# Column-group matmuls for the first MLP layer and the query projection of a decode block

## The chip, the cores and the metric

The kernel runs on one core of a Trainium2 chip. The metric is the device time of one execution in microseconds (us), the median of several executions. The span that a profile covers is about 1.8 us shorter than the time (133.4 against 135.22 us for the profiled run of the kernel before), because the time also includes a start and an end.

The words used below: PE is the matrix engine, DVE the vector engine, ACT the scalar engine, POOL a further engine that hardly works here; SP issues the large loads. HBM is the large memory that the DMA engines read from, SBUF the memory on the core that they write to, PSUM the memory that receives the results of matmuls. A matmul has a stationary operand, which is loaded into PE first (a weight load), and a moving operand, whose columns are then streamed through. The granted clock is the share of its full clock that PE was given, as the profile records it.

## The reference

One token (a row of 576 numbers) goes through two branches, and a gate mixes them:

```python
q = x @ wq                               # [576] x [576, 4096], 32 heads of 128
k, v = k_cache[:, :, -4096:], v_cache[:, :, -4096:]   # 16 heads x 4096 x 128, bf16
p = softmax(q k^T / sqrt(128))           # two query heads share one k/v head
a = (p v) @ wo                           # [4096] x [4096, 576]
h = gelu(x @ w1 + b1)                    # [576] x [576, 4608]
b = h @ w2 + b2                          # [4608] x [4608, 576]
g = sigmoid(sum(x * gate_w))
out = g * a + (1 - g) * b
```

Each weight is used once and each cache entry for two query heads at once, so no load can be saved by reuse. The windows of K and V are 2 x 16 x 4096 x 128 x 2 bytes = 33.6 MB, the four weight matrices 20.1 MB. The profile shows 53.62 MB read from HBM.

## The kernel before

All large loads are issued in order from one engine (SP) into a few large buffers, which are tagged A to D and used again:

```python
w1_t = big.tile([P, NI, FH], ..., tag="B")      # 3 DMAs, 5.3 MB
wq_t = big.tile([P, NI, QH], ..., tag="A")      # 3 DMAs, 4.7 MB
# ...
for g in range(NG):
    k_t = big.tile([P, 2, SL, Dh], ..., tag="CDBA"[g])   # K group 2 needs w1's buffer, group 3 wq's
    # ... per half group: DVE transposes 128x2048 twice into kt (2 buffers), PE 16 score matmuls
# ...
w2_t = big.tile([P, NF, D], ..., tag="B")       # first half of w2: needs K group 2 transposed
# v_t tags "CDAC"[g], wo_t tag "D", second half of w2 into w2_t
```

In MLP layer 1 the weight is the stationary operand and x the moving one. The 576 rows of w1 are cut into two halves of 2304 columns, which gives 1152 half rows, 9 (NI) on each partition. Column t of `x2[:, i, :]` holds x on those partitions whose half row i belongs to half t, and zeros elsewhere. The result lands on the partitions directly:

```python
h_ps = ps_m.tile([P, NF], FP32, name="h_ps", tag="m")
for j in range(NJ):                       # 18 bias matmuls
    nc.tensor.matmul(h_ps[:, j:NF:NJ], lhsT=b1_t[:, j:FH:NJ], rhs=ident[0:2, 0:2], ...)
for i in range(NI):
    for j in range(NJ):                   # 9 x 18 = 162 weight loads, 2 moving columns each
        nc.tensor.matmul(h_ps[:, j:NF:NJ], lhsT=w1_t[:, i, j:FH:NJ], rhs=x2[:, i, :], ...)
# ... gelu on h_ps
for i in range(NI):
    for j in range(Hq // 2):              # 9 x 16 = 144 for q, the same way
        nc.tensor.matmul(q_ps[:, j : Hq : Hq // 2], lhsT=wq_t[:, i, j * Dh : (j + 1) * Dh], rhs=x2[:, i, :], ...)
nc.vector.tensor_copy(out=q_b[:], in_=q_ps[:])
# ... 4 matmuls and 4 copies scatter q_b into the block-diagonal qz_flat, then the K stage starts
```

## Time and profile before

| | before |
|---|---|
| time, median of 3 | 135.37 us (135.1 to 135.47) |
| HBM read | 53.62 MB |
| DMA share of the chain that ended last | 71% |
| PE busy | 81.0 us, 61% of the span |
| MLP layer 1 on PE | 10.4 to 21.8 us |
| first K transpose on DVE | 30.70 us |

The first view is the profile page of the kernel before: the span in 40 slices of 3.3 us (busy tenths of PE, the granted PE clock in tenths, busy tenths of the 16 DMA engines, GB/s moved), then the chain of work that ended last, by engine and by line.

```profile
PE   0239999260957778768789185008923955296771
...
PEclk9999999999999999999999968655555555555798
DMA  4999999999999999999999999999998999999970
GB/s 137 416 437 419 422 452 400 415 418 442 432 413 437 417 435 418 432 427 405 435 444 474 442 393 418 472 432 393 432 467 373 403 408 441 407 420 422 408 266 0
...
DMA 71%; DVE 10%; ACT 7%; PE 6%; issue 2%; SPq 1%; DVEq 0%
DMA k_t<-in_A_k_cache_dram 25%; DMA w_t<-in_B_w_dram 18%; DMA wq_t<-in_A_wq_dram 15%; DMA v_t<-in_A_v_cache_dram 13%; ACT p_t L356 7%; DVE kt L305 5%; PE o_ps L400 3%; DVE pt L364 2%; DVE m L326 2%; PE s_ps L314 1%; SPq L281 1%; PE q_ps L242 1%; PE t_ps L382 0%; PE mb_ps L343 0%; DVE out_row L435 0%
```

The chain is mostly the DMA of K, w1 and w2 (both printed as w_t), wq and V; PE has 6% of it. GB/s stays between about 370 and 475 whether PE is busy or not. The clock row needs care: the first record of the granted clock in this trace is at 36.6 us, and slices before it are printed as full. The distance of the score matmuls' starts says otherwise: 427 ns before that record and 217 ns after it. So the scores from 33.1 us up to that record ran at the half clock; what the clock was before them, this trace does not show.

The second view is the busy time by stage, kernel before: start and end of the stage in us, its length, then busy time of PE, PE weight loads, DVE, ACT and POOL, each with its number of instructions, then granted clock, DMA share and GB/s.

```profile
core 0: us, PE busy (x) PEld busy (x) DVE busy (x) ACT busy (x) POOL busy (x), PEclk, DMA share, GB/s
...
4.00:16.00 12.00, 7.98 (x105) 6.83 (x106) 4.91 (x36) 0.17 (x1) 0.00 (x0) 1.00 1.01 427
16.00:32.00 16.00, 10.19 (x241) 9.96 (x241) 3.83 (x12) 0.75 (x3) 0.00 (x0) 1.00 1.01 423
32.00:76.00 44.00, 31.90 (x128) 12.59 (x127) 37.16 (x18) 0.00 (x0) 0.00 (x0) 1.00 1.01 430
...
92.00:112.00 20.00, 12.72 (x449) 12.27 (x447) 0.00 (x0) 0.00 (x0) 0.00 (x0) 0.50 0.99 418
112.00:128.00 16.00, 10.01 (x117) 5.90 (x118) 0.48 (x2) 0.00 (x0) 0.00 (x0) 0.58 1.01 419
```

In none of these stages does the DMA share leave 0.99 to 1.01. PE is busy for 18 of 28 us from 4 to 32 us; the last column shows that the data come at the same rate in these stages as in the others.

The third view is the timeline of PE, kernel before, from 9 to 32 us: start, length, line, operation, number of instructions, and in brackets the idle time before and what ended it.

```profile
10.35 1.27 PE L192 MATMUL h_ps<-ident,rows 2*128 2x2 bf16 x18
11.56 10.21 PE L204 MATMUL h_ps<-x,w_t 128*128 128x2 bf16 x162
21.63 1.42 PE L242 MATMUL q_ps<-x,wq_t 128*128 128x2 bf16 x48
...
28.18 1.01 PE L242 MATMUL q_ps<-x,wq_t 128*128 128x2 bf16 x32 [0.61 <-DMA wq_t<-in_A_wq_dram]
```

These are the bias, w1 and q matmuls that the change replaces: 1.27 + 10.21 us, and for q 4.3 us, of which the last third waits for the last piece of wq and starts at 28.18 us.

The fourth view is the timeline of DVE, kernel before.

```profile
29.23 0.19 DVE L251 CAST q_b<-q_ps 128x32 bf16<-128x32 f32 x1 [5.15 <-PE q_ps L242]
...
30.70 4.76 DVE L305 STREAM_TRANSPOSE kt<-k_t 128x2048 f32<-128x2048 f32 x2
38.06 4.50 DVE L305 STREAM_TRANSPOSE kt<-k_t 128x2048 f32<-128x2048 f32 x2 [2.59 <-DMA k_t<-in_A_k_cache_dram]
```

After q is copied, the first two K transposes run at once; the third waits 2.59 us for its K data. That wait is the slack of the q path at this point.

### The profile page before, as it was taken

To read this page: it belongs to the slowest core of one execution; us is meant where nothing else is said; L and a number is where in the kernel's file an instruction comes from. 1 tells how busy PE (TensorE), PEld (TensorE's weight loads), DVE (VectorE), ACT (ScalarE), POOL (GpSimd) and SP (SyncE) were. 2 spreads that over 40 slices of the span, in tenths; PEclk is the share of its full clock that TensorE was granted. 3 is DMA by queue.
4 is the path that set the end of the run, shared out by engine and by line. 5 is a ranking of instruction groups with operands and counts; after the bars stand their busy time and mean duration, and the time that the engine had idled before them with its cause. 6 is when DMAs were issued, how large, how long until landed. Compare 5 with 4: busy or idle time off the path is not lost.

```text
span 133.4 us, 2466 instructions
## 1 busy us (share of the span) xinstructions
PE 81.0 (61%) x1126; PEld 52.5 (39%) x1126; DVE 56.0 (42%) x83; ACT 12.3 (9%) x22; POOL 0.7 (1%) x6
## 2 busy tenths in 40 slices
PE   0239999260957778768789185008923955296771
PEld 0118998250323223323333042008922954143340
DVE  6277003118658988988994710663000000100001
ACT  3000000001000000000000059930000000000001
POOL 2000000000000000000000000000000000000000
PEclk9999999999999999999999968655555555555798
DMA  4999999999999999999999999999998999999970
GB/s 137 416 437 419 422 452 400 415 418 442 432 413 437 417 435 418 432 427 405 435 444 474 442 393 418 472 432 393 432 467 373 403 408 441 407 420 422 408 266 0
DMA packets 4486, 53.78 MB, mean 403 GB/s; under 512 B 502, under 2 KB 762, under 8 KB 1020
## 3 DMA queue, kind: packets, MB, share of 16 engines
q1 hardware_dynamic: 4466, 53.61, 95.5%
q8 instruction: 9, 0.15, 0.5%
q10 hardware_dynamic: 10, 0.01, 0.0%
q14 instruction: 1, 0.01, 0.0%
HBM read 53.62 MB, written 0.00 MB: 402 GB/s over the span
## 4 chain that ended last, share of the span: by engine, by line
DMA 71%; DVE 10%; ACT 7%; PE 6%; issue 2%; SPq 1%; DVEq 0%
DMA k_t<-in_A_k_cache_dram 25%; DMA w_t<-in_B_w_dram 18%; DMA wq_t<-in_A_wq_dram 15%; DMA v_t<-in_A_v_cache_dram 13%; ACT p_t L356 7%; DVE kt L305 5%; PE o_ps L400 3%; DVE pt L364 2%; DVE m L326 2%; PE s_ps L314 1%; SPq L281 1%; PE q_ps L242 1%; PE t_ps L382 0%; PE mb_ps L343 0%; DVE out_row L435 0%
## 5 line engine op out<-in xcount | busy, mean ns | idle before, releaser
L314 PE MATMUL s_ps<-kt,qz_flat 128*128 128x512 bf16 x128 | 31.9, 393 | 11.9 <-DVE kt L305 11.9
L305 DVE STREAM_TRANSPOSE kt<-k_t 128x2048 f32<-128x2048 f32 x16 | 36.0, 2291 | 4.9 <-DMA k_t<-in_A_k_cache_dram 4.7
L314 PEld LDWEIGHTS <-qz_flat 128*128 128x128 bf16 x128 | 12.7, 99 | 30.7 <-issue 16.8
L400 PE MATMUL o_ps<-pt,v_t 128*128 128x8 bf16 x512 | 14.9, 168 | 7.9 <-DMA v_t<-in_A_v_cache_dram 4.5
L400 PEld LDWEIGHTS <-v_t 128*128 128x128 bf16 x512 | 14.5, 105 | 8.5 <-DMA v_t<-in_A_v_cache_dram 4.9
L356 ACT ACTIVATE p_t<-s_ps,negm 128x512 bf16<-128x512 f32 x8 | 9.7, 1414 | 47.2 <-DVE negm L347 47.2
L204 PE MATMUL h_ps<-x,w_t 128*128 128x2 bf16 x162 | 10.2, 202 | 0.0
L204 PEld LDWEIGHTS <-w_t 128*128 128x128 bf16 x162 | 10.1, 163 | 0.0
L178 PE MATMUL y_ps<-wo_t,ov 128*1 128x288 bf16 x64 | 7.7, 430 | 3.6 <-DMA wo_t<-in_A_wo_dram 3.6
L418 DVE TENSOR_TENSOR om<-o_ps,rgh 128x128 bf16<-128x128 f32 x1 | 0.3, 292 | 22.0 <-PE o_ps L400 22.0
L178 PE MATMUL y_ps<-w_t,gt 128*1 128x288 bf16 x72 | 7.2, 343 | 1.9 <-DMA w_t<-in_B_w_dram 1.8
L364 DVE STREAM_TRANSPOSE pt<-p_t 128x2048 bf16<-128x2048 bf16 x2 | 4.6, 2312 | 7.4 <-ACT p_t L356 7.4
L435 DVE CAST out_row<-y_ps 1x288 bf16<-1x288 f32 x1 | 0.4, 446 | 16.0 <-PE y_ps L178 16.0
L178 PEld LDWEIGHTS <-ov 128*1 128x1 bf16 x64 | 4.0, 119 | 7.1 <-issue 3.6
L242 PE MATMUL q_ps<-x,wq_t 128*128 128x2 bf16 x144 | 4.3, 166 | 3.3 <-DMA wq_t<-in_A_wq_dram 3.3
L382 PE MATMUL t_ps<-ls,ones 128*128 128x32 f32 x2 | 0.6, 396 | 8.9 <-DVE ls L380 8.9
L178 PEld LDWEIGHTS <-gt 128*1 128x1 bf16 x72 | 3.7, 98 | 4.9 <-issue 2.8
L242 PEld LDWEIGHTS <-wq_t 128*128 128x128 bf16 x144 | 4.1, 104 | 3.4 <-DMA wq_t<-in_A_wq_dram 3.4
L434 ACT CAST out_row<-y_ps 1x288 bf16<-1x288 f32 x1 | 0.4, 390 | 42.9 <-PE y_ps L178 42.9
L213 DVE COPY hacc<-h_ps 128x36 f32<-128x36 f32 x1 | 0.2, 196 | 9.4 <-PE h_ps L204 9.4
L382 PEld LDWEIGHTS t_ps<-ls,ones 128*128 128x128 f32 x2 | 0.5, 310 | 9.2 <-issue 9.2
L105 PE MATMUL xs_ps<-one_b,rows 1*128 1x1 bf16 x9 | 0.7, 195 | 4.0 <-DVE rows L102 4.0
(69 smaller groups left out, 28.8 us busy)
## 6 DMA issues: line engine op xcount, KB each, us to landing
k_t<-in_A_k_cache_dram SPq DMA_DIRECT2D x6, 2048.0 KB, 31.6
v_t<-in_A_v_cache_dram SPq DMA_DIRECT2D x3, 4096.0 KB, 29.9
w_t<-in_B_w_dram SPq DMA_DIRECT2D x3, 1728.0 KB, 10.5
k_t<-in_A_k_cache_dram SPq DMA_DIRECT2D x4, 1024.0 KB
wo_t<-in_A_wo_dram SPq DMA_DIRECT2D x2, 1728.0 KB
w_t<-in_B_w_dram SPq DMA_DIRECT2D x1, 2592.0 KB
wq_t<-in_A_wq_dram SPq DMA_DIRECT2D x1, 2048.0 KB
v_t<-in_A_v_cache_dram SPq DMA_DIRECT2D x1, 2048.0 KB
```

Source lines behind the costliest of these rows:

```text
L105: nc.tensor.matmul(xs_ps[:, i : i + 1], lhsT=xdup[:, i : 2 * D : NI], rhs=one_b[0:1, 0:1], start=(i == 0), stop=(i == NI - 1), skip_group_ ...
L178: nc.tensor.matmul(y_out[s], lhsT=vec, rhs=row[:, s * DH : (s + 1) * DH], start=start, stop=stop, skip_group_check=True,)
L204: nc.tensor.matmul(h_ps[:, j:NF:NJ], lhsT=w1_t[:, i, j:FH:NJ], rhs=x2[:, i, :], start=False, stop=(i == NI - 1 and j == NJ - 1), skip_grou ...
L242: nc.tensor.matmul(q_ps[:, j : Hq : Hq // 2], lhsT=wq_t[:, i, j * Dh : (j + 1) * Dh], rhs=x2[:, i, :], start=(i == 0 and j == 0), stop=(i ...
L281: nc.sync.dma_start(out=tile_[:, c0 : c0 + n, :].rearrange("p c d -> p (c d)"), in_=src[:, :, c0 * Dh : (c0 + n) * Dh],)
L305: nc.vector.transpose(out=kt[:, u * half : (u + 1) * half].bitcast(FP32), in_=k_t[:, f, u * SL // 2 : (u + 1) * SL // 2, :] .rearrange("p ...
L314: nc.tensor.matmul(s_ps[:, u * 512 : (u + 1) * 512].rearrange("p (c k) -> p c k", k=32), lhsT=qz[:, h0 // 2, j, :], rhs=kv[:, u * SL // 4 ...
L326: nc.vector.reduce_max(out=m2[:], in_=s_ps[:].rearrange("p (n b) -> p b n", b=2), axis=AX.X)
L356: nc.scalar.activation(out=p_t[:, cs, :, b], in_=s_ps[:].rearrange("p (c k u b) -> p u b c k", k=8, u=2, b=2)[:, f, b % 2], func=ACT.Exp, ...
L364: nc.vector.transpose(out=pt[:, cs, :].rearrange("p c h -> p (c h)"), in_=p_t[:, cs, :, :].rearrange("p c k b -> p (c k b)"),)
L382: nc.tensor.matmul(t_ps[:], lhsT=ones[:], rhs=ls[:], start=True, stop=True)
L400: nc.tensor.matmul(o_ps[:, 8 * g : 8 * g + 8, 0], lhsT=v_t[:, c, :], rhs=pt[:, c, 8 * g : 8 * g + 8], start=(c == 0), stop=(c == NCK - 1),)
```

## The change

The intent is to swap the operands. x, padded from 2 to 32 columns with zeros, becomes the stationary operand, and the weight moves through PE in pieces of 512 columns, four of them at once in the four column groups of the array. So 306 weight loads of 128x128 become 90 of 128x32. The result then lies as rows: the column group u has two useful rows, on partitions 32u and 32u + 1. Copies to SBUF and small matmuls against selected columns of the identity turn it onto the partitions again, in fp32 for h and in bf16 for q.

```diff
-    x2 = const.tile([P, NI, 2], BF16, name="x2")
+    x2 = const.tile([P, NI, 32], BF16, name="x2")
+    nc.vector.memset(x2[:], 0.0)
 ...
+    hq_ps = ps_s.tile([P, 3, 512], FP32, name="hq_ps", tag="s_ps")
+    def h_add(vec, row, start=False, stop=False):
+        rv = row.rearrange("p (q j) -> p q j", j=NJ)
+        for n in range(6):
+            u = n % 4
+            nc.tensor.matmul(
+                hq_ps[32 * u : 32 * u + 32, n // 4, 0 : (512 if n < 4 else P)],
+                lhsT=vec,
+                rhs=rv[:, :, 4 * u : 4 * u + 4] if n < 4 else rv[:, :, 16 + u],
+                start=start, stop=stop, tile_position=(0, 32 * u), ...)
+    h_add(ident[0:2, 0:32], b1_t, start=True)
+    for i in range(NI):
+        h_add(x2[:, i, :], w1_t[:, i, :], stop=(i == NI - 1))
+    h_sb = const.tile([P, 512], FP32, name="h_sb")
+    nc.vector.tensor_copy(out=h_sb[:], in_=hq_ps[:, 0, :])
+    hb_sb = const.tile([64, P], FP32, name="hb_sb")
+    nc.scalar.copy(out=hb_sb[:], in_=hq_ps[0:64, 1, 0:P])
+    selv = ident_f[:].rearrange("p (u t) -> p t u", u=4)
+    for j in range(4):
+        nc.tensor.matmul(h_ps[:, :, j:16:4], lhsT=h_sb[:, j:512:4], rhs=selv[:, 0:2, :], ...)
+    nc.tensor.matmul(h_ps[:, :, 16:18], lhsT=hb_sb[:], rhs=selv[0:64, 0:2, 0:2], ...)
 ... (the 18 + 162 matmuls into h_ps go)
-        for j in range(Hq // 2):
+        for u in range(4):
             nc.tensor.matmul(
-                q_ps[:, j : Hq : Hq // 2],
-                lhsT=wq_t[:, i, j * Dh : (j + 1) * Dh],
-                rhs=x2[:, i, :],
+                hq_ps[32 * u : 32 * u + 32, 2, :],
+                lhsT=x2[:, i, :],
+                rhs=wq_t[:, i, 512 * u : 512 * u + 512],
+                tile_position=(0, 32 * u), ...)
+    q_sb = const.tile([P, 512], BF16, name="q_sb")
+    nc.scalar.copy(out=q_sb[:], in_=hq_ps[:, 2, :])
+    for a in range(4):
+        nc.tensor.matmul(q_ps[:, :, :, a], lhsT=q_sb[:, a * Dh : (a + 1) * Dh], rhs=sel8, ...)
-    nc.vector.tensor_copy(out=q_b[:], in_=q_ps[:])
+    nc.scalar.copy(out=q_b[:], in_=q_ps[:].rearrange("p t u a -> p (t u a)"))
```

Of a row of w1, the columns of h are taken with step 18 (`rv`), so the moving operand of h is read in runs of 4 elements (8 bytes) every 36 bytes, and for the last two pieces (128 columns) in single elements every 36 bytes. The moving operand of q is contiguous. No load, no load buffer and no order of loads is changed. (The new sums `hq_ps` lie in the PSUM buffer of the scores, which the scores need only after q has been copied out of it.)

More of the change, by code (lines that the diff above doesn't have):

```diff
@@ L187 @@
     y_add(ones[0:1, 0:1], b2g[0:1, :], start=True)
-    h_ps = ps_m.tile([P, NF], FP32, name="h_ps", tag="m")
-    for j in range(NJ):
+    hq_ps = ps_s.tile([P, 3, 512], FP32, name="hq_ps", tag="s_ps")
[7 more added lines that the diff above has]
+                rhs=rv[:, :, 4 * u : 4 * u + 4] if n < 4 else rv[:, :, 16 + u],
+                start=start,
+                stop=stop,
+                tile_position=(0, 32 * u),
+                skip_group_check=True,
+            )
+    h_add(ident[0:2, 0:32], b1_t, start=True)
+    qz_flat = const.tile([P, Hkv // 2 * 516 + 128], BF16, name="qz_flat")
+    nc.vector.memset(qz_flat[:].bitcast(FP32), 0.0)
+    for i in range(NI):
[4 more added lines that the diff above has]
+    nc.scalar.copy(out=hb_sb[:], in_=hq_ps[0:64, 1, 0:P])
+    h_ps = ps_m.tile([P, 2, NJ], FP32, name="h_ps", tag="m")
+    selv = ident_f[:].rearrange("p (u t) -> p t u", u=4)
+    for j in range(4):
         nc.tensor.matmul(
-            h_ps[:, j:NF:NJ],
-            lhsT=b1_t[:, j:FH:NJ],
-            rhs=ident[0:2, 0:2],
+            h_ps[:, :, j:16:4],
+            lhsT=h_sb[:, j:512:4],
+            rhs=selv[:, 0:2, :],
             start=(j == 0),
@@ L199 @@
         )
-    qz_flat = const.tile([P, Hkv // 2 * 516 + 128], BF16, name="qz_flat")
-    nc.vector.memset(qz_flat[:].bitcast(FP32), 0.0)
-    for i in range(NI):
-        for j in range(NJ):
-            nc.tensor.matmul(
-                h_ps[:, j:NF:NJ],
-                lhsT=w1_t[:, i, j:FH:NJ],
-                rhs=x2[:, i, :],
-                start=False,
-                stop=(i == NI - 1 and j == NJ - 1),
-                skip_group_check=True,
-            )
+    nc.tensor.matmul(
+        h_ps[:, :, 16:18],
+        lhsT=hb_sb[:],
+        rhs=selv[0:64, 0:2, 0:2],
+        start=False,
+        stop=True,
+        skip_group_check=True,
+    )
     hacc = const.tile([P, NF], FP32, name="hacc")
-    nc.vector.tensor_copy(out=hacc[:], in_=h_ps[:])
+    nc.vector.tensor_copy(out=hacc[:], in_=h_ps[:].rearrange("p t j -> p (t j)"))
     z2 = const.tile([P, NF], FP32, name="z2")
@@ L236 @@
     nc.vector.tensor_scalar(out=gt[:], in0=p1[:], scalar1=omg[:, 0:1], scalar2=None, op0=ALU.mult)
-    q_ps = ps_m.tile([P, Hq], FP32, name="q_ps", tag="m")
     for i in range(NI):
-        for j in range(Hq // 2):
+        for u in range(4):
             nc.tensor.matmul(
-                q_ps[:, j : Hq : Hq // 2],
-                lhsT=wq_t[:, i, j * Dh : (j + 1) * Dh],
-                rhs=x2[:, i, :],
-                start=(i == 0 and j == 0),
-                stop=(i == NI - 1 and j == Hq // 2 - 1),
+                hq_ps[32 * u : 32 * u + 32, 2, :],
+                lhsT=x2[:, i, :],
+                rhs=wq_t[:, i, 512 * u : 512 * u + 512],
+                start=(i == 0),
+                stop=(i == NI - 1),
+                tile_position=(0, 32 * u),
                 skip_group_check=True,
             )
+    q_sb = const.tile([P, 512], BF16, name="q_sb")
+    nc.scalar.copy(out=q_sb[:], in_=hq_ps[:, 2, :])
+    q_ps = ps_m.tile([P, 2, 4, 4], FP32, name="q_ps", tag="m")
+    sel8 = ident[:].rearrange("p (u t) -> p t u", u=4)[:, 0:2, :]
+    for a in range(4):
+        nc.tensor.matmul(
+            q_ps[:, :, :, a],
+            lhsT=q_sb[:, a * Dh : (a + 1) * Dh],
+            rhs=sel8,
+            start=(a == 0),
+            stop=(a == 3),
+            skip_group_check=True,
+        )
     q_b = const.tile([P, Hq], BF16, name="q_b")
-    nc.vector.tensor_copy(out=q_b[:], in_=q_ps[:])
+    nc.scalar.copy(out=q_b[:], in_=q_ps[:].rearrange("p t u a -> p (t u a)"))
     qj_ps = ps_m.tile([P, 4, Hkv // 2, 4], FP32, name="qj_ps", tag="m")
@@ L285, in load @@
             c0 += n
-    s_ps = ps_s.tile([P, SL * 32], FP32, name="s_ps")
+    s_ps = ps_s.tile([P, SL * 32], FP32, name="s_ps", tag="s_ps")
     for g in range(NG):
```

## The prediction

> **What bounds the kernel now.** The DMA stream. In the page's slices the DMA engines are at 9 tenths or more from slice 2 to 38; in the table by stage their share stays between 0.91 and 1.09 in every 4 us from 4 to 128 us, at 385 to 460 GB/s. The Trainium skill, "DMA: Bandwidth & Descriptors", section "Where 436 GB/s comes from", names about 435 GB/s as the ceiling; this trace sits just under it. The chain of waits agrees: 71% DMA, 6% PE. The last weights land at 130.3 us, with about 3 us of tail.
>
> **Removed** (groups of instructions): 162 w1 matmuls with their own weight loads (63 ns apart, 10.2 us busy, ending at 21.8 us), 18 bias matmuls (1.3 us), 144 q matmuls (4.3 us).
>
> **Added.** 60 column-group matmuls for w1 and bias (40 of 512 columns, 20 of 128), 36 of 512 columns for q, 9 selector matmuls, a 128x512 copy on DVE, copies on ACT, one memset. That column groups overlap shows before: the 288-column output matmuls in two groups start 1 to 4 ns apart, pairs following every 240 ns at half clock. Score matmuls of 512 columns follow every 427 ns (first ones) or 217 (full clock). So I estimate one row of w1 at 427 + 107 = 0.53 us at half clock: MLP layer 1 with bias about 5.3 us of PE instead of 11.5, q about 3.9 at most; half of each at full clock. The w1 pieces land until about 15 us, so the MLP should end near 17.
>
> **On the critical path: almost nothing.** The freed buffers let K groups 2 and 3 be issued; but data queued ahead of them lasts until about 46 and 56 us (bytes landed over time), and they were issued before 34. Earlier issue lengthens the queue, not the rate. q stays gated by its last piece (28.1 us in the chain). After it the path gets longer: before, q's copy at 29.23; now a 128x512 PSUM copy on ACT (estimate 0.6 us), selector matmuls (0.3), an ACT copy (0.25), so the first K transpose comes 1 to 1.4 us later (30.7 to about 32). The third transpose waited 2.6 us for K data at 35.5 us, which absorbs it; the K stage still ends when its last piece lands (62.6) plus transposes, about 73.5. Softmax, V, output projection and the last w2 piece are unchanged.
>
> **Predicted time.** 135.3 us, 8 in 10 within 134.7 to 135.9. Faster by over 2%: 0.02; within 2%: 0.95; slower by over 2%: 0.03.
>
> **What would show the steps.** DMA share near 1.0 from 4 to 128 us, same bytes; chain about 70% DMA, ending on w2 and the output row. PE busy falls by 7 to 12 us. Fours of 512-column matmuls start a few ns apart, 217 or 427 ns between fours; if serial, the MLP ends near 25 us, still hidden. First K transpose near 32 us, the third still at about 38.
>
> **What would make it wrong.** The granted clock: before, records begin at 36.6 us (full), fall to half at about 78, return to full near 125. Denser early matmuls may move this. Half clock during the scores would put PE at 6.8 us per K piece against 4.9 of DMA, delaying softmax and the fourth V load (issued 95.9, with about 5 us of queue left): 10 us of delay would cost some 5. Half clock at the end costs only about 0.2. A strided moving read (8-byte runs, 36 bytes apart) slower than one column per cycle would hide in over 20 us of slack.

## The result and the profile after

| | before | after |
|---|---|---|
| time, median of 4 runs each | 135.28 us (135.1 to 135.47) | 135.19 us (135.09 to 135.39) |
| ratio | | 0.9995, 95% interval 0.9976 to 1.0014 |
| PE busy | 81.0 us | 79.9 us |
| weight loads busy | 52.5 us | 43.7 us |
| h ready (its copy on DVE) | 21.80 us | 21.19 us |
| first K transpose | 30.70 us | 31.96 us |
| mean granted clock (profiled run) | 0.829 | 0.757 |

The time is the same. The slices and the chain of the page, kernel after:

```profile
PE   0229877261698787778789187007852955296571
...
PEclk9999985555569999999999955955555555555899
DMA  4999999999999999999999999999999999999960
...
DMA 71%; DVE 10%; ACT 7%; PE 6%; issue 2%; SPq 1%; DVEq 0%
```

The DMA row is as full as before, and the shares of the chain by engine are the same figures. What moved is the clock row: records now begin at 15.3 us with full clock, then half from 18.7 to 39.2 us (slices 6 to 12).

The busy time by stage, kernel after:

```profile
4.00:16.00 12.00, 6.97 (x57) 3.19 (x58) 5.02 (x37) 0.17 (x1) 0.00 (x0) 1.00 1.00 426
16.00:32.00 16.00, 9.14 (x72) 4.66 (x71) 3.07 (x12) 1.56 (x6) 0.00 (x0) 0.58 1.01 425
32.00:76.00 44.00, 32.50 (x128) 12.75 (x128) 38.07 (x17) 0.22 (x1) 0.00 (x0) 0.92 1.01 430
```

From 4 to 32 us the PE busy time fell from 18.2 to 16.1 us with 129 matmuls instead of 346. DMA share and GB/s did not move.

The timeline of PE, kernel after:

```profile
11.43 4.01 PE L197 MATMUL hq_ps<-w_t,x 128*32 128x512 bf16 x36
16.03 1.72 PE L197 MATMUL hq_ps<-w_t,x 128*32 128x512 bf16 x18 [0.59 <-DMA w_t<-in_B_w_dram]
18.63 2.01 PE L219 MATMUL h_ps<-ident_f,h_sb 128*128 128x8 f32 x8 [0.88 <-DVE h_sb L213]
20.56 0.59 PE L227 MATMUL h_ps<-ident_f,hb_sb 64*128 64x4 f32 x2
...
28.45 1.04 PE L264 MATMUL hq_ps<-wq_t,x 128*32 128x512 bf16 x8 [0.61 <-DMA wq_t<-in_A_wq_dram]
30.18 0.28 PE L278 MATMUL q_ps<-ident,q_sb 128*128 128x8 bf16 x4 [0.69 <-ACT q_sb L274]
```

The merged lines for w1 are named by their first member, the 512-column form, and hold the 128-column form as well. Six of nine rows of x take 4.01 us (0.64 us each), then PE waits for the third piece of w1 until 16.03. The sums are complete at about 17.75 us, four us earlier than before (11.56 + 10.21 = 21.77). Then the result is turned: a copy on DVE, and after it ten records of fp32 selector matmuls (each of the five matmuls of the source shows as two), which last until 21.15 us. The copy and these matmuls together give 3.4 of the four us back.

The timelines of ACT and DVE, kernel after:

```profile
29.54 0.59 ACT L274 CAST q_sb<-hq_ps 128x512 bf16<-128x512 f32 x1 [7.21 <-PE hq_ps L264]
...
31.96 4.51 DVE L341 STREAM_TRANSPOSE kt<-k_t 128x2048 f32<-128x2048 f32 x2
...
38.31 4.50 DVE L341 STREAM_TRANSPOSE kt<-k_t 128x2048 f32<-128x2048 f32 x2 [1.84 <-DMA k_t<-in_A_k_cache_dram]
```

Between the last q matmul and the first K transpose there is now a PSUM copy of 0.59 us, selector matmuls and another copy. The first transposes start 1.26 us later; the third starts at 38.31 us against 38.06, again released by its data, after a shorter wait (1.84 us).

### The profile page after: what moved, and what is told of

Read it like the earlier page. It is cut to its first block, busy times and chain, and to the rows that moved or that the text cites. A ratio compares the mean times of both kernels' runs of the same rounds, so it can differ in the third digit from the quotient of the medians.

```text
span 133.6 us, 2043 instructions
## 1 busy us (share of the span) xinstructions
PE 79.9 (60%) x912; PEld 43.7 (33%) x912; DVE 56.5 (42%) x84; ACT 13.3 (10%) x25; POOL 0.7 (1%) x6
## 3 DMA queue, kind: packets, MB, share of 16 engines
HBM read 53.62 MB, written 0.00 MB: 401 GB/s over the span
## 4 chain that ended last, share of the span: by engine, by line
DMA 71%; DVE 10%; ACT 7%; PE 6%; issue 2%; SPq 1%; DVEq 0%
DMA k_t<-in_A_k_cache_dram 25%; DMA w_t<-in_B_w_dram 18%; DMA wq_t<-in_A_wq_dram 16%; DMA v_t<-in_A_v_cache_dram 12%; ACT p_t L392 7%; DVE kt L341 5%; PE o_ps L436 3%; DVE pt L400 2%; DVE m L362 2%; PE s_ps L350 1%; SPq L317 1%; PE hq_ps L264 1%; PE t_ps L418 0%; PE mb_ps L379 0%; PE mt_ps L367 0%
## 5 line engine op out<-in xcount | busy, mean ns | idle before, releaser
L350 PE MATMUL s_ps<-kt,qz_flat 128*128 128x512 bf16 x128 | 32.5, 399 | 10.3 <-DVE kt L341 10.3
L179 PE MATMUL y_ps<-wo_t,ov 128*1 128x288 bf16 x64 | 7.2, 409 | 3.7 <-DMA wo_t<-in_A_wo_dram 3.7
L179 PE MATMUL y_ps<-w_t,gt 128*1 128x288 bf16 x72 | 7.9, 364 | 2.4 <-DMA w_t<-in_B_w_dram 2.3
L264 PE MATMUL hq_ps<-wq_t,x 128*32 128x512 bf16 x36 | 4.4, 623 | 4.0 <-DMA wq_t<-in_A_wq_dram 4.0
L197 PE MATMUL hq_ps<-w_t,x 128*32 128x512 bf16 (+1 forms) x54 | 5.7, 509 | 0.6 <-DMA w_t<-in_B_w_dram 0.6
L301 DVE CAST qz_flat<-qj_ps 32x128 bf16<-32x128 f32 x2 | 0.6, 284 | 7.9 <-PE qj_ps L290 7.6
L197 PEld LDWEIGHTS <-x 128*32 128x32 bf16 x54 | 2.3, 116 | 4.1 <-issue 2.8
L264 PEld LDWEIGHTS <-x 128*32 128x32 bf16 x36 | 1.2, 123 | 6.3 <-issue 6.3
```

The lines of the kernel that those rows point to most:

```text
L179: nc.tensor.matmul(y_out[s], lhsT=vec, rhs=row[:, s * DH : (s + 1) * DH], start=start, stop=stop, skip_group_check=True,)
L197: nc.tensor.matmul(hq_ps[32 * u : 32 * u + 32, n // 4, 0 : (512 if n < 4 else P)], lhsT=vec, rhs=rv[:, :, 4 * u : 4 * u + 4] if n < 4 else ...
L264: nc.tensor.matmul(hq_ps[32 * u : 32 * u + 32, 2, :], lhsT=x2[:, i, :], rhs=wq_t[:, i, 512 * u : 512 * u + 512], start=(i == 0), stop=(i = ...
L350: nc.tensor.matmul(s_ps[:, u * 512 : (u + 1) * 512].rearrange("p (c k) -> p c k", k=32), lhsT=qz[:, h0 // 2, j, :], rhs=kv[:, u * SL // 4 ...
```

## The experiments

The theory: the stream of 53.62 MB bounds the time, so what PE does before 32 us is hidden as long as it frees its buffers and delivers q before certain times. The rival: the PE saving was worth something, and the longer path from q to the scores took it away. A zero that is the sum of two effects looks like a zero of none, so the two parts have to be run alone.

Eight kernels ran. The first four shared 11 runs of the kernel before (median 135.48 us), the last four 7 runs on another chip (135.53 us).

### 1. The MLP part alone

```diff
 # changed kernel, q as before
-                hq_ps[32 * u : 32 * u + 32, 2, :], lhsT=x2[:, i, :], rhs=wq_t[:, i, 512 * u : ...]
+                q_ps[:, j : Hq : Hq // 2], lhsT=wq_t[:, i, j * Dh : (j + 1) * Dh], rhs=x2[:, i, 0:2]
```

> The change for MLP layer 1 alone, q as before. Theory (DMA stream bounds all, early PE work is hidden): time within 0.3% of both kernels (135.0 to 135.5 us), first K transpose back at about 30.7 us, the fused copy of h still near 21 us. Rival (the PE gain was real and the longer q tail of about 1.3 us took it back): faster than before by 0.5 to 1.3 us.

Measured: 135.43 us (6 runs), ratio 0.9991, interval 0.9970 to 1.0013. The first transpose was at 30.66 us, the copy of h at 21.18. Nothing was gained that q's tail could have taken back; the interval leaves room for 0.4 us at most, and the rival asked for 0.5 to 1.3. The granted clock was 0.95 instead of 1.00 in the K stage of this run (40 to 70 us), and the score matmuls followed every 223 instead of 217 ns; the time did not notice.

### 2. The q part alone

```diff
 # changed kernel, MLP layer 1 as before (162 matmuls into h_ps, lhsT=w1_t, rhs=x2[:, i, 0:2])
```

> The change for q alone, MLP layer 1 as before. Theory: within 0.3% again, first K transpose near 32 us, third K transpose still near 38 us because it waits for its data. Rival (gain and loss cancel): slower than before by about 1.3 us (136.5 us).

Measured: 135.45 us (6 runs), ratio 0.9986, interval 0.9963 to 1.0009. The first transpose came at 31.72, the third at 38.06 us, exactly where it was before. The rival's 136.5 is ruled out: the tail of 1 us costs nothing. Each half of the change is zero by itself, within the 0.4 to 0.5 us that the intervals leave.

### 3. Fewer bytes

```diff
-    for i0, i1 in ((0, 3), (3, 6), (6, NI)):
+    for i0, i1 in ((0, 3), (3, 6)):                        # third piece of w1 not loaded
-        h_add(x2[:, i, :], w1_t[:, i, :], ...)
+        h_add(x2[:, i, :], w1_t[:, min(i, 5), :], ...)     # wrong result on purpose
```

> The changed kernel without the load of the third piece of w1 (1.77 MB of 53.6; its rows are computed from another row, so the result is wrong on purpose; the instructions are the same otherwise). Theory: the stream runs at about 0.42 MB per us, so 4.2 us are saved: about 131.0 us. Rival (the chain of PE, ACT and DVE work from q through softmax bounds the time by itself): clearly less, 0 to 2 us.

Measured: 131.37 us (4 runs), ratio 0.9695, interval 0.9667 to 0.9722; wrong result, as intended. 1.77 MB less is 4.1 us less (135.48 - 131.37), that is 0.43 MB per us, about the rate of the stream. The instructions on PE, ACT and DVE were all still there, so no chain of them bounds the time by itself.

### 4. The selector matmuls in bf16

```diff
-    h_sb = const.tile([P, 512], FP32, name="h_sb")
+    h_sb = const.tile([P, 512], BF16, name="h_sb")
-    hb_sb = const.tile([64, P], FP32, name="hb_sb")
+    hb_sb = const.tile([64, P], BF16, name="hb_sb")
-    selv = ident_f[:].rearrange(...)
+    selv = ident[:].rearrange(...)
```

> The changed kernel with the h copies and the selector matmuls in bf16 instead of fp32. The ten fp32 selector records took 2.6 us together (0.234 us apart); in bf16, with five records, they should take about 0.3 us like q's four (0.03 to 0.05 us apart), so h comes out near 19 us instead of 21.2 and the PE busy time falls by about 2.3 us. Time by theory unchanged, 135.0 to 135.5 us; a rival in which the selectors ate a real gain says 1 to 2 us faster.

Measured: 135.52 us (4 runs), ratio 0.9997, interval 0.9969 to 1.0025; the result was still correct. The timeline of this kernel:

```profile
18.73 0.30 PE L219 MATMUL h_ps<-ident,h_sb 128*128 128x8 bf16 x4 [0.80 <-DVE h_sb L213]
...
19.02 0.18 PE L227 MATMUL h_ps<-ident,hb_sb 64*128 64x4 bf16 x1
...
19.24 0.20 DVE L236 COPY hacc<-h_ps 128x36 f32<-128x36 f32 x1 [0.56 <-PE h_ps L227]
```

The selectors take about 0.5 us instead of 2.6, and h is copied at 19.24 us, 2 us earlier. So the fp32 selectors ate 2 of the 3.4 us that the turn gave back, and the time did not care whether they were eaten. PE busy fell from 79.9 to 76.6 us, more than the 2.1 us of the selectors; the granted clock was also full at 19.9 to 20.7 us, where q's first twelve matmuls took 0.83 instead of 1.47 us.

### 5 to 7. q made late on purpose

```diff
-    nc.scalar.copy(out=q_sb[:], in_=hq_ps[:, 2, :])
+    for _ in range(7):       # 18 and 31 in the other two
+        nc.scalar.copy(out=q_sb[:], in_=hq_ps[:, 2, :])
```

If time is hidden because there is slack, the slack must have an end. One ACT copy takes 0.59 us and they follow every 0.62 us, so this delays q by a known amount and changes nothing else in the source. The order of the instructions on DVE did change, as the traces below show.

> The changed kernel with the copy of q out of PSUM on ACT done 7 times instead of once (0.59 us each), so q and the first K transpose come about 3.6 us later (35.6 us). Theory (slack): the 12th transpose, which frees the buffer for the first half of w2, would end at 59.0 + 3.6 = 62.6 us against 62.3 now, and the queue still holds K data until about 65.9, so the time stays within 0.4 us. Rival (the tail from q into the scores is on the critical path): plus 3.6 us.

> The same with 18 copies, about 10.4 us later. Theory: the 12th transpose ends near 69.4 us; w2 is then issued about 5 us after the point (64.5 us) at which the queue runs dry, so a hole of some 5 us opens in the DMA stream after the K data and the time grows by 4 to 7 us. Rival: plus 10.4 us. If the slack is larger than I think: 0.

> The same with 31 copies, about 18.4 us later. Theory: beyond the slack of about 5.5 us every further us costs one: plus 11.5 to 15 us; between 18 and 31 copies the slope is 0.9 to 1.1 us per us. Rival: plus 18.4.

| copies | extra delay of q | time (4 runs each) | ratio, 95% interval | first half of w2 issued at (profile) |
|---|---|---|---|---|
| 1 (the change, its own rounds) | 0 | 135.19 us | 0.9995, 0.9976 to 1.0014 | 62.56 us |
| 7 | 3.7 us | 135.64 us | 1.0008, 0.9980 to 1.0036 | 62.05 us |
| 18 | 10.5 us | 138.11 us | 1.0176, 1.0138 to 1.0214 | 65.83 us |
| 31 | 18.5 us | 145.71 us | 1.0765, 1.0712 to 1.0819 | 74.22 us |

(Extra delay is the number of extra copies times 0.617 us. The profiles of these runs are single executions, with spans of 133.7, 135.7 and 144.7 us; the times are medians of four.) Two of these issues, first of the changed kernel, then with 31 copies:

```profile
62.56 0.34 SPq L408 DMA_DIRECT2D w_t<-in_B_w_dram  x1
```

```profile
74.22 0.33 SPq L409 DMA_DIRECT2D w_t<-in_B_w_dram  x1
```

With 7 copies the DVE timeline is:

```profile
30.42 2.31 DVE L342 STREAM_TRANSPOSE kt<-k_t 128x2048 f32<-128x2048 f32 x1 [6.89 <-DMA k_t<-in_A_k_cache_dram]
...
35.14 2.31 DVE L342 STREAM_TRANSPOSE kt<-k_t 128x2048 f32<-128x2048 f32 x1
37.80 4.50 DVE L342 STREAM_TRANSPOSE kt<-k_t 128x2048 f32<-128x2048 f32 x2 [0.35 <-DMA k_t<-in_A_k_cache_dram]
...
57.52 4.50 DVE L342 STREAM_TRANSPOSE kt<-k_t 128x2048 f32<-128x2048 f32 x2 [0.40 <-DMA k_t<-in_A_k_cache_dram]
```

The first transpose did not come at 35.6 us, as expected, but at 30.42 us: it now stands ahead of q's scatter on DVE, which came at 34.22 us, 3.2 us later than in the changed kernel. The second transpose starts at 35.14 us, 0.9 us later than there (34.20), and nothing after it is late: the third waits for its data still, for 0.35 us. The rival's 3.6 us does not appear. How much of the delay the old order would have absorbed, this run does not show.

With 18 copies I had expected 4 to 7 us more and got 2.6 (138.11 - 135.53). The DVE timeline tells why:

```profile
30.60 2.31 DVE L342 STREAM_TRANSPOSE kt<-k_t 128x2048 f32<-128x2048 f32 x1 [7.25 <-DMA k_t<-in_A_k_cache_dram]
33.10 2.31 DVE L342 STREAM_TRANSPOSE kt<-k_t 128x2048 f32<-128x2048 f32 x1 [0.18 <-DMA k_t<-in_A_k_cache_dram]
...
48.14 26.43 DVE L342 STREAM_TRANSPOSE kt<-k_t 128x2048 f32<-128x2048 f32 x12 [1.52 <-PE s_ps L351]
```

When q comes this late, two transposes stand ahead of q's scatter on DVE (one with 7 copies, four with 31); the order was chosen when the program was built. They don't need q, so DVE had done 4.6 us of its work before q arrived. The delay was absorbed in part, which I had not looked up in the order of instructions before running. DVE cannot run further ahead than two half groups, because `kt` has two buffers: the fifth transpose starts at 48.14 us, released by the first score matmuls, which need q (with 31 copies at 56.53 us, in the same way). So past this point the delay passes from q through the scores to the transposes.

With 31 copies I had expected 11.5 to 15 us more, and it was 10.2 (145.71 - 135.53), also outside the range, although the slope between the two runs came as expected. The delay less its cost is 7.9 us with 18 copies and 8.3 with 31; the slack of the path as it then stood was about 8 us, not 5.5.

What goes with the lost time is the issue of w2's first half. Its buffer is free when the twelfth transpose has read K group 2. This issue waited 4.6 us for transposes in the changed kernel and 16.6 us with 31 copies. Kernel with 31 copies, by stage, 2 us each:

```profile
64.00:66.00 2.00, 1.71 (x9) 0.69 (x8) 2.00 (x2) 0.00 (x0) 0.00 (x0) 1.00 0.70 291
66.00:68.00 2.00, 1.71 (x9) 0.68 (x8) 2.00 (x2) 0.00 (x0) 0.00 (x0) 1.00 0.03 12
68.00:70.00 2.00, 1.70 (x9) 0.67 (x7) 2.00 (x2) 0.00 (x0) 0.00 (x0) 1.00 0.00 0
70.00:72.00 2.00, 1.75 (x8) 0.67 (x7) 2.00 (x2) 0.00 (x0) 0.00 (x0) 1.00 0.00 0
72.00:74.00 2.00, 1.89 (x8) 0.77 (x8) 2.00 (x1) 0.00 (x0) 0.00 (x0) 1.00 0.04 8
...
76.00:78.00 2.00, 1.70 (x9) 0.71 (x8) 2.00 (x2) 0.00 (x0) 0.00 (x0) 1.00 0.71 301
```

The DMA share falls to zero for 8 us: the K data are in, and nothing else was issued. This is what a critical delay looks like, and neither the change nor the kernel before has it. The issue of w2 was 11.7 us later than in the changed kernel (74.22 - 62.56) and the span 11.1 us longer (144.7 - 133.6); with 18 copies, 3.3 and 2.1 us (span 135.7). By the medians the time grew by 10.2 and 2.6 us. So at this gate the stream forgives about 1 us of lateness (0.6 to 1.5 by these figures) and then charges about one for one. From 18 to 31 copies, 8.0 us of delay cost 7.6 us (145.71 - 138.11), a slope of 0.95.

### 8. The same columns, read contiguously

```diff
-                rhs=rv[:, :, 4 * u : 4 * u + 4] if n < 4 else rv[:, :, 16 + u],
+                rhs=row[:, 512 * n : 512 * n + 512] if n < 4 else row[:, 2048 + P * u : 2048 + P * u + P],
```

> The changed kernel with w1 and b1 read by the column-group matmuls in contiguous runs of 512 and 128 columns (the result is wrong on purpose, since the columns of h land in other places). Now one row of w1 takes 0.64 us at the half clock and 0.52 at the full one. If the strided reading costs it: 0.53 us (640 columns) at the half clock and 0.27 at the full. If it is the order of six instructions in one queue: 0.64 at the half clock still, and 0.32 at the full. Time unchanged either way.

Measured: one look, 135.12 us (one run, state unknown; the profile is of another execution, span 134.1 us), wrong result as intended. The groups of PE instructions while the clock is still low (11.3 to 15.2 us; number, busy us, mean ns), first of the kernel after, then of the contiguous one:

```profile
L197 PE MATMUL hq_ps<-w_t,x 128*32 128x512 bf16 x24 | 3.8, 613 | 0.0
L197 PE MATMUL hq_ps<-w_t,x 128*32 128x128 bf16 x12 | 2.5, 410 | 0.0
```

```profile
L196 PE MATMUL hq_ps<-w_t,x 128*32 128x512 bf16 x24 | 3.3, 630 | 0.0
L196 PE MATMUL hq_ps<-w_t,x 128*32 128x128 bf16 x12 | 1.9, 314 | 0.0
```

The 128-column matmuls take 314 instead of 410 ns; the means of the 512-column ones hardly differ. The distance of starts is clearer than these durations. From the start times in the trace, one row of w1 (four matmuls of 512 and two of 128 columns) follows the one before after:

```
                 half clock    full clock
strided (after)    0.640 us      0.52 us
contiguous         0.533 us      0.271 us
```

(At the full clock the changed kernel's own trace has only two such distances, 0.50 and 0.52; run 3 has three of 0.52.) Contiguous reading gives the two numbers that the column count asks for: 640/512 of the 427 and 217 ns of a score matmul are 534 and 271 ns. Strided reading costs 20% at the half clock, and takes nearly the whole advantage of the full clock away (0.52 against 0.27). So it is the reading and not the order of six instructions. The starts within a column group say which reading: the 128 single elements take 0.235 us instead of 0.107 at the half clock, which is the whole loss there, and 0.215 instead of 0.055 at the full clock; the 512 columns in runs of 4 are as fast as contiguous ones at the half clock and take 0.30 instead of 0.215 us at the full clock. The one timed run gives no sign that this matters for the time of this kernel.

## Why the prediction was right, point by point

- **The bound (right).** The DMA stream. The K stage ran at 430 GB/s in the mean before and after, close to the 435 that the Trainium skill names as the fabric ceiling in "DMA: Bandwidth & Descriptors", section "Where 436 GB/s comes from". The same section says that for loads from HBM a limit of about 358 binds; these loads on one core passed it. ("9 tenths or more from slice 2 to 38" overlooked one 8.) The bound was shown from both sides: 1.77 MB fewer is 4.1 us fewer (3), and a hole in the stream, empty for 8 us and thin beside that, goes with 10.2 us more (7), while PE work removed or added in the first 32 us costs nothing (1, 2, 4).
- **The time (right).** 135.3 us was said, 135.19 measured.
- **Column groups overlap (right for q).** The first four of q's 512-column matmuls start 3 to 4 ns apart, and fours follow every 427 ns, as single score matmuls do at the half clock. That is the "up to 4x" of the Trainium skill, "TensorEngine Tiling (Array Packing)", section "Theoretical Speedup".
- **The size of the MLP part on PE (partly wrong).** I had 0.53 us for a row of w1, and it was 0.64, because of the strided reading, which I had named as a risk and not costed. "The MLP should end near 17" holds for the sums (17.75 us) only. The term that I left out of the sum are the fp32 selectors for h: I costed the selectors of q (0.3 us, and 0.28 came), and let h's pass at the same price. They took 2.6 us, so that h was ready only at 21.2 us.
- **"PE busy falls by 7 to 12 us" (wrong).** It fell by 1.1 us. Replaced were 15.8 us (10.2 + 1.3 + 4.3). Added were about 5.7 us for w1, about 1.2 for the bias, 4.4 for q, 2.6 + 0.3 for selectors, which is 14.2, a difference of 1.6 us; and the score matmuls took 0.6 us longer (32.5 against 31.9), as they ran at the half clock until about 39 us instead of 36.6. These sum to about 1.0. I had set a short estimate against the measured time of the old part, without the turn.
- **q later by 1 to 1.4 us, absorbed by the third transpose's wait (right).** 1.26 us, and the third transpose at 38.31 us against 38.06. Run 5 made q 3.2 us later still without a loss, but with one transpose moved ahead of q, so it does not measure this slack in the order as it was.
- **The risk in a late K stage (right in kind, wrong in place).** I had named the fourth V load, with about 5 us of queue left, as the first thing to come too late. Runs 6 and 7 show that it is the first half of w2, which waits for the twelfth transpose, and that it has about 1 us to spare. That the change did not come near it is due to the K data, which release the transposes, and not to this margin.
- **The clock (right that it may move; luck that it came back in time).** Full clock was granted from 15.3 us for 3.4 us, then half until 39.2. Half clock during the scores was named as what could cost about 5 us; nothing in the prediction said that it would end after the first 12 of 128 score matmuls, as it did. Runs 1 and 2 have mean clocks of 0.744 and 0.832 in their profiles and the same time.
- **Over 20 us of slack for freed buffers.** This was only argued from bytes landed over time; no run delayed the MLP alone, so the figure stays an estimate.

No version that beats both kernels is pointed to by these runs. While the stream runs, only fewer bytes or a faster stream would help, as run 3 shows, and every byte is needed once; the start and the 3 us after the last landing were not looked into; run 4's version is the leanest on PE and has the same time.

## What to carry to other kernels

Before tuning an engine, read the DMA share of the stage in which it works: where it stays at 1.0 and the issues run ahead of the data, an engine's time there is worth nothing, however large its busy share looks. When two halves of a change can cancel, run each alone, and prove the slack by using it up: a delay that costs nothing, then one that costs one for one. Look then whether the delayed program still has the order of the old one; here it did not. And when operands are swapped so that the result has to be turned, count the turn and the reading pattern of the new moving operand; here the turn, a copy and five tiny fp32 matmuls, gave back 3.4 of the four us by which the sums came earlier.

## What the Trainium skill lacked or had wrong

- "TensorEngine Tiling (Array Packing)", section "Theoretical Speedup", gives up to 4x for four column groups, with nothing about how the moving operand lies in memory. Contiguous, the trace agrees. With 8-byte runs every 36 bytes and single elements every 36 bytes, a row of 640 columns took 0.64 instead of 0.533 us at the half clock and 0.52 instead of 0.271 us at the full clock. That reads of SBUF should hit a line of 16 bytes at least twice is stated on the page "SBUF — State Buffer", section "Specifications (TRN2)"; the single elements, one to a line here, were indeed the slow ones at both clocks. What both pages lack is the cost in a matmul.
- "FP8 and Floating Point Precision", section "TensorE Precision Notes", says that true fp32 takes 4 passes. The section has no time for it. The trace shows two records for each fp32 selector matmul, 0.234 us apart at the half clock and 0.233 at the full clock (run 3), with weight loads of about 0.33 us. Four of these matmuls took 2.01 us in fp32 and 0.30 us in bf16, a ratio of 6.7, more than the 4 passes. The weight loads were busy for 1.94 of the 2.01 us, so they probably set the pace; no run tests this alone.
- "TensorE: Matmul & The Clock Gate", section "What's actually happening", says that the granted ratio is 4/8 or 8/8 only; its section "Seeing it yourself" adds 13/16 for three or more busy cores of a die. One run here (run 1), on one core, was granted 0.95 wherever the others were granted 1.00, and the distance of the score matmuls in the K stage grew from 217 to 223 ns with it.
